# VectorE's exponentials taken from the score tile's third bank, in five passes instead of six

## The chip, the core and the metric

The kernel runs on one core of a Trainium2 chip. The profile names the core's engines PE (TensorE, matrix products; its weight loads are listed apart as PEld), DVE (VectorE), ACT (ScalarE), POOL (GpSimd) and SP (SyncE, which issues the DMAs here). Each engine works through its own list of instructions in order, and the lists are tied together by semaphores: an instruction can carry a wait for another engine's count.

The metric is the device time of one execution in microseconds (us), as the median of three runs. One further execution was recorded by the profiler. Its span is the time from its first to its last instruction, and all durations below come from it.

## The reference

One layer of a transformer over 2,048 tokens of width 640: attention with 32 heads of 20 columns, then a gated product of two linear maps, each behind a layer norm and added to its input. All tensors are bfloat16.

```python
def _A_ref(x, wqkv, wo):
    B, S, D = x.shape            # 1, 2048, 640
    H = 32
    Dh = D // H                  # 20
    q, k, v = ...                # from x @ wqkv, each (B, H, S, Dh)
    scores = jnp.einsum("bhqd,bhkd->bhqk", q, k) * (Dh ** -0.5)
    p = _softmax(scores, axis=-1)
    o = jnp.einsum("bhqk,bhkd->bhqd", p, v)
    return o.transpose(0, 2, 1, 3).reshape(B, S, D) @ wo

def _B_ref(x, w_gate, w_up, w_down):
    return ((x @ w_gate) * (x @ w_up)) @ w_down

h = x + _A_ref(_layernorm(x), A_wqkv, A_wo)
h2 = h + _B_ref(_layernorm(h), B_w_gate, B_w_up, B_w_down)
```

For each head there are 2,048 x 2,048 scores, and each needs an exponential. That is the bulk of the elementwise work.

## The kernel before

**Tiling of the attention.** Scores are computed transposed: 128 keys on the partitions, queries along the columns. Heads go in groups of four (`HPG`), eight groups (`NG`). The four heads of a group lie on four bands of 32 partitions (`SLOT`), so a score product uses 32 rows of the array, and a product with the values writes 32 columns of it. A *segment* (`segs`, L294 to L303) is one group of heads against a block of queries: passes "0", "1", "2" and "3" have 512 queries, passes "A" and "B" 256. For the first four groups of pass "0" the keys come in four chunks (kinds "copy", "add" and "last"); every other segment takes all 16 key blocks in one go (kind "only"). There are 50 segments: 16 chunked ones, 20 unchunked ones of passes "0" to "2", and 14 of passes "3", "A" and "B".

**Score tiles.** The units of work (a key block, a head, 512 or 256 queries) are packed one behind the other into tiles of three banks, 3 x 512 = 1,536 columns (`tiles`, L311 to L324). For tile number i, `emit_S(i)` (L417) writes the scores into a tile `sc` of the pool `scp`, which has two buffers, and then issues one ACTIVATE on ScalarE that turns all 1,536 columns into exponentials in a bfloat16 tile `E` (L433). The finished units join a queue `av_q`, from which `emit_AV` (L568) takes four at a time (eight of 256 columns) and multiplies them with the values into the accumulator `acc` (L597). A column of ones in the values yields the sums of the softmax.

**The main loop** (L1071 to L1100) runs once per tile. It emits, in this order: the scores and exponential of tile i; up to `BUDGET` = 640 ns of the current job's matmuls (`go_on`); the products with the values of a tile some places back; due events and small VectorE work; VectorE's passes for its own exponentials (`step_x`); and, if no job was under way, the start of another job (`begin`). Jobs are the projections to q, k and v, the output projection, the gated product and its down projection. They come from a list in order and write into the one-buffer tile `mi` (`bank()`, L243). The planner keeps an estimate of VectorE's backlog in `now["dve"]`: each instruction adds its supposed cost, and every tile takes `STEP` = 1,331 ns off.

**VectorE's exponentials.** For each of the 20 segments in `X_SEGS` the units of key block 2 are left out of the tile list (L315). Their scores, 80 units of 512 columns, are made apart by `emit_x` (L443) with a matmul into `mi` (L453), in places where a job would otherwise have begun (L1096). VectorE then computes the exponential in six passes: a scaled conversion to an integer that holds exponent and mantissa in its bits (L463), two bit operations that part them (L474, L475), and three multiply-and-add passes (L476, L477, L468). The result `xe` joins `av_q` when all four heads of the segment are done (`put_x`). `need_x` (L496) makes what is missing before a segment closes.

**The constant in the exponent.** A spare row of q and k adds the constant `SHIFT` to all scores. It cancels in the softmax; it places the scores where VectorE's bit arithmetic needs them, and the bias of the ACTIVATE (`EXP_BIAS`) takes it out again. At the end `flag_ok` (L1043) tests the sums' least and greatest value and a saturating conversion, and on a bad outcome the branch `general` computes everything again in a safe way.

Of the kernel before, what the change touches and what calls it, by code (L numbers as in the profile page):

```python
# [3 lines left out]

# [6 lines left out]
BF16 = mybir.dt.bfloat16  # L11
F32 = mybir.dt.float32
I32 = mybir.dt.int32
ACT = mybir.ActivationFunctionType
ALU = mybir.AluOpType
AX = mybir.AxisListType

P = 128
# [26 lines left out]
EPS_B = 1.0013580322265625e-05  # L45
SUM_LO = 1e-15
SUM_HI = 1e15
NEXT = "next slot"
END = "end"
BUDGET = 640  # L50
# [2 lines left out]
LAG = 10  # L53
STEP = 1331
AUX_LOAD, X_LOAD = 1200, 900
SHIFT = 394.0
X_AHEAD, X_STEP, X_OUT = 8, 5, 6
LOG2E = 1.4426950408889634
X_SCALE = SM_SCALE * LOG2E * 2.0 ** 23
C3 = 0.07802454279127117  # L60
X_P, X_Q, X_R = -0.10261439735317812, 6.123365857342997, 5.794771205884579
EXP_BIAS = (SHIFT * SM_SCALE * LOG2E - 127.0) / LOG2E - math.log(C3) - SHIFT * SM_SCALE


@with_exitstack
def kernel(
# [197 lines left out]
    def q_of(g, b, c0, w):  # L264
        return qb[g][:, c0:c0 + w] if b == NB - 1 else qa[g][:, b * QB + c0:b * QB + c0 + w]
# [30 lines left out]
    for ch in range(NB):  # L296
        for g in range(G1):
# [28 lines left out]
    first_tile = {}  # L326
    for i, (us, _) in enumerate(tiles):
        for s, *_ in us:
            first_tile.setdefault(s, i)
    x_todo = deque((first_tile[s] - X_AHEAD + X_STEP * j, s, j) for s in X_SEGS for j in range(HPG))  # L330
    x_pieces = deque()
    x_made = {}
    x_put = []
    x_live = {"units": 0, "passes": 0}

    av_q = deque()
    acc = {"seg": None, "t": None, "from": 0, "left": 0}
# [79 lines left out]
    def emit_S(i):  # L417
        sc = scp.tile([P, EW], F32, name="sc")
        us, n = tiles[i]
        for s, kt, j, _ in us:  # L420
            p, g = segs[s][0:2]
            ensure(("k", g, kt // TPB))
            ensure(("q", PASS[p][0], g))
        for s, kt, j, o in us:
            p, g = segs[s][0:2]
            b, c0, w = PASS[p]
            nc.tensor.matmul(  # L427
                sc[:, o:o + w],
                lhsT=kT[g][SLOT * j:SLOT * (j + 1), kt * P:(kt + 1) * P],
                rhs=q_of(g, b, c0, w)[SLOT * j:SLOT * (j + 1), :],  # L430
                start=True, stop=True)
        e = ep.tile([P, EW], BF16, name="E")
        nc.scalar.activation(e[:, 0:n], sc[:, 0:n], ACT.Exp, bias=EXP_BIAS, scale=SM_SCALE)  # L433
        for s, kt, j, o in us:
            av_q.append((i, s, kt, j, e[:, o:o + PASS[segs[s][0]][2]]))

    def x_ready():
        due, s, _ = x_todo[0]
        p, g = segs[s][0:2]
        return (due <= now["i"] and x_live["units"] < X_OUT and x_live["passes"] < 2  # L440
                and ("q", PASS[p][0], g) in done and ("k", g, 0) in done)

    def emit_x():  # L443

        _, s, j = x_todo.popleft()
        p, g = segs[s][0:2]
        b, c0, w = PASS[p]
        n = BANK // w
        ensure(("k", g, X_KT // TPB))
        ensure(("q", b, g))  # L450
        ps = bank()
        for k in range(n):
            nc.tensor.matmul(  # L453
                ps[:, k * w:(k + 1) * w],
                lhsT=kT[g][SLOT * j:SLOT * (j + 1), (X_KT + k) * P:(X_KT + k + 1) * P],
                rhs=q_of(g, b, c0, w)[SLOT * j:SLOT * (j + 1), :],
                start=True, stop=True)
        v = xp.tile([P, BANK], I32, name="xv", bufs=2)
        m = xp.tile([P, BANK], F32, name="xm")
# [3 lines left out]
        nc.vector.tensor_scalar(v[:], ps[:], X_SCALE, 0.0, ALU.mult, ALU.max)  # L463
        x_live["units"] += 1
        x_live["passes"] += 1

        def last():
            nc.vector.scalar_tensor_tensor(e[:], t[:], X_R, v[:].bitcast(F32), ALU.add, ALU.mult)  # L468
            x_live["passes"] -= 1
            x_made.setdefault(s, []).append((j, e))  # L470
            if len(x_made[s]) == HPG:
                x_put.append([(now["i"], s, X_KT + k, j, e[:, k * w:(k + 1) * w]) for k in range(n) for j, e in x_made[s]])
        x_pieces.extend([
            (430, lambda: nc.vector.tensor_scalar(m[:].bitcast(I32), v[:], 0x007FFFFF, 0x3F800000, ALU.bitwise_and, ALU.bitwise_or)),  # L474
            (430, lambda: nc.vector.tensor_scalar(v[:], v[:], 0x7F800000, None, ALU.bitwise_and)),  # L475
            (690, lambda: nc.vector.scalar_tensor_tensor(t[:], m[:], X_P, m[:], ALU.add, ALU.mult)),  # L476
            (690, lambda: nc.vector.scalar_tensor_tensor(t[:], t[:], X_Q, m[:], ALU.add, ALU.mult)),  # L477
            (690, last)])

    def put_x():  # L480

# [7 lines left out]
    def step_x(n):  # L489
        while n > 0 and x_pieces:  # L490
            ns, fn = x_pieces.popleft()
            dve(ns)
            fn()
            n -= 1

    def need_x(s):  # L496
        while len(x_made.get(s, ())) < HPG:
            if x_pieces:
                step_x(1)
                continue  # L500
            while not cur["fresh"]:
                step()
            emit_x()

    def norm(s, asb):
        p, g = segs[s][0:2]
# [61 lines left out]
    def emit_AV(upto):  # L568
# [21 lines left out]
            return  # L590
        for _ in range(ready):
            _, _, kt, j, e = av_q.popleft()
            if s in X_SEGS and kt == X_KT:
# [448 lines left out]

    def flag_ok():  # L1043
        n = col["n"]
        nc.vector.tensor_reduce(ext[:, 0:1], sums_all[:, 0:n], axis=AX.X, op=ALU.min)
        nc.vector.tensor_reduce(ext[:, 1:2], sums_all[:, 0:n], axis=AX.X, op=ALU.max)
        lo = small.tile([P, 1], F32, name="lo", tag="m32")
        hi = small.tile([P, 1], F32, name="hi", tag="rstd")
        nc.vector.tensor_scalar(lo[:], ext[:, 0:1], SUM_LO, None, ALU.is_ge)
        nc.vector.tensor_scalar(hi[:], ext[:, 1:2], SUM_HI, None, ALU.is_le)  # L1050
        ok = small.tile([P, 1], BF16, name="ok", tag="den")
        nc.vector.tensor_tensor(ok[:], lo[:], hi[:], ALU.mult)
        top = small.tile([P, 1], I32, name="top", tag="nt")
        nc.vector.tensor_scalar(top[:], huge[:], 1.0, 0.0, ALU.mult, ALU.max)
        nc.vector.tensor_scalar(lo[:], top[:], 2.0e9, None, ALU.is_ge)
        nc.vector.tensor_tensor(ok[:], ok[:], lo[:], ALU.mult)
        return ok

# [10 lines left out]
    b_seen, a_seen = 0, False  # L1069
    i = 0  # L1070
    while i < n_tiles or av_q:  # L1071
        now["i"], now["dve"] = i, max(0, now["dve"] - STEP)
        if i < n_tiles:
            emit_S(i)
        if i == first_last:
            for g in range(NG):
                ensure(("spill", g))
# [15 lines left out]
        while x_pieces and now["dve"] < X_LOAD:  # L1093
            step_x(1)
        if not used:
            if x_todo and cur["fresh"] and now["dve"] < X_LOAD and x_ready():  # L1096
                emit_x()
# [106 lines left out]
```

## Time and profile before

| | us |
|---|---|
| median of three runs | 981.02 (979.47 to 981.46) |
| span of the profiled execution | 977.6 |
| TensorE matmuls busy | 865.3 |
| VectorE busy | 576.8 |
| ScalarE busy | 905.2 |
| first exponential starts / last one ends, from the span's start | 16.1 / 933.6 |
| VectorE, six passes of 80 units: L463, L474, L475, L476, L477, L468 | 55.0, 37.4, 35.1, 55.7, 56.3, 56.6 |

A row of the profile's list of groups reads: line, engine, operation, tile written <- tiles read, partitions x elements and type of both, count | total busy us, mean ns of one | idle time of the engine just before them, and whose work ended it. Busy time counts overlapping instructions once, so with the exponentials, which overlap, total busy time is less than count times mean. In the views in order of time a row starts with its start and its length in us, and equal instructions that follow each other are merged into one row with a count.

### The profile page before, as it was taken

The page shows a single profiled execution, that of the slowest core. Times are in us where ns is not written, and L with a number is a line of the kernel's source. Part 1 is how long each engine was busy: PE and PEld are TensorE (multiplying, and loading weights), DVE is VectorE, ACT ScalarE, POOL GpSimd, SP SyncE. Part 2 cuts the span into 40 slices and gives each one's busy share as a digit, 9 for nine tenths or more (in the row PEclk, how much of TensorE's full clock was granted, in tenths as well). Part 3 has the DMA queues.
Part 4 walks back from the last instruction along what each step waited for, and adds up shares of the span by engine and source line. Part 5 has one row for each costly group of instructions (what it writes and reads, how often), then busy time and mean ns, then how long its engine had stood idle before and what let it go on. Part 6 is the DMA issues. An engine that isn't in the chain of part 4 may idle for free.

```text
span 977.6 us, 17623 instructions
## 1 busy us (share of the span) xinstructions
PE 865.3 (89%) x6981; PEld 325.1 (33%) x7041; DVE 576.8 (59%) x1186; ACT 905.2 (93%) x692; POOL 64.6 (7%) x163
## 2 busy tenths in 40 slices
PE   6779998889989899999898988898889999989987
PEld 4223332222223222233232222233332333435455
DVE  7564367877777777777677677777143331143232
ACT  6689999999999899999999999999899999999941
POOL 4110001200000000000000000000000000000000
PEclk9999999999999599999778899999597999989989
DMA  6000000010014022101420222000602000211210
GB/s 182 4 24 1 1 25 24 13 32 27 5 47 146 12 66 59 40 13 33 180 67 12 66 67 60 12 22 23 163 1 66 14 13 20 67 36 40 81 35 17
DMA packets 67816, 44.42 MB, mean 45 GB/s; under 512 B 18504, under 2 KB 63404, under 8 KB 67728
## 3 DMA queue, kind: packets, MB, share of 16 engines
q1 hardware_dynamic: 67728, 43.23, 15.5%
q8 instruction: 57, 0.93, 0.4%
q14 instruction: 31, 0.25, 0.1%
HBM read 35.91 MB, written 7.30 MB: 44 GB/s over the span
## 4 chain that ended last, share of the span: by engine, by line
ACT 44%; PE 32%; issue 13%; DVE 9%; POOL 1%; ACTq 0%; DVEq 0%; POOLq 0%
ACT E L433 44%; PE sc L427 8%; PE acc L597 6%; PE mi L878 3%; PE mi L270 3%; PE mi L812 2%; PE mi L284 2%; PE mi L911 2%; PE f L878 2%; DVE xv L463 1%; PE mi L453 1%; DVE st L176 1%; PE f L911 1%; PE mi L252 1%; DVE vx L239 1%
## 5 line engine op out<-in xcount | busy, mean ns | idle before, releaser
L433 ACT ACTIVATE E<-sc 128x1536 bf16<-128x1536 f32 x656 | 887.8, 1662 | 30.4 <-PE sc L427 29.7
L427 PE MATMUL sc<-qa,kT 32*128 32x512 bf16 x1456 | 205.9, 406 | 41.3 <-ACT E L433 35.0
L597 PE MATMUL acc<-E,vx 128*32 128x512 bf16 (+1 forms) x2352 | 215.6, 374 | 5.3 <-DVE vx L239 4.1
L427 PEld LDWEIGHTS <-kT 32*128 32x128 bf16 x2352 | 89.8, 92 | 260.8 <-issue 251.0
L597 PEld LDWEIGHTS <-vx 128*32 128x32 bf16 x2432 | 56.6, 94 | 159.7 <-issue 151.9
L270 PE MATMUL mi<-lnT,wp 128*128 128x512 bf16 x282 | 84.7, 382 | 9.7 <-DVE kT L277 2.3
L427 PE MATMUL sc<-qb,kT 32*128 32x256 bf16 (+1 forms) x896 | 72.0, 301 | 13.8 <-ACT E L433 13.0
L529 POOL TENSOR_TENSOR on<-asb,bc 128x512 bf16<-128x512 f32 (+1 forms) x30 | 34.5, 1150 | 714.7 <-DMA bc<-scr 507.1
L463 DVE TENSOR_SCALAR xv<-mi 128x512 int32<-128x512 f32 x80 | 55.0, 688 | 29.9 <-PE mi L453 26.3
L911 PE MATMUL mi<-wd,hh 128*128 128x320 bf16 x378 | 68.4, 303 | 3.6 <-DVE xv L463 3.5
L239 DVE CAST u<-mi 128x512 bf16<-128x512 f32 (+3 forms) x56 | 34.9, 624 | 56.2 <-PE mi L878 56.0
L886 DVE TENSOR_TENSOR hh<-mi,u 128x512 bf16<-128x512 f32 (+3 forms) x56 | 34.9, 624 | 55.0 <-PE mi L878 54.9
L878 PE MATMUL mi<-ln2T,wu 128*128 128x512 bf16 (+2 forms) x188 | 55.2, 385 | 4.6 <-DVE xv L463 3.0
L468 DVE SCALAR_TENSOR_TENSOR xe<-xt,xv 128x512 bf16<-128x512 f32 x80 | 56.6, 707 | 2.0
L477 DVE SCALAR_TENSOR_TENSOR xt<-xt,xm 128x512 f32<-128x512 f32 x80 | 56.3, 704 | 0.9
L476 DVE SCALAR_TENSOR_TENSOR xt<-xm 128x512 f32<-128x512 f32 x80 | 55.7, 697 | 0.0
L878 PE MATMUL mi<-ln2T,wg 128*128 128x512 bf16 (+2 forms) x187 | 52.3, 372 | 2.2 <-issue 0.8
L911 PEld LDWEIGHTS <-hh 128*128 128x128 bf16 x448 | 37.5, 97 | 40.1 <-issue 29.8
L915 DVE TENSOR_TENSOR xr<-mi,xr 128x320 bf16<-128x320 f32 x27 | 13.3, 492 | 51.3 <-PE mi L911 51.3
L812 PE MATMUL mi<-wo,on 128*128 128x320 bf16 x224 | 41.8, 311 | 0.7 <-DVE xv L463 0.4
L607 DVE COPY asb<-acc 128x512 f32<-128x512 f32 (+1 forms) x34 | 20.2, 594 | 34.5 <-PE acc L597 32.3
L277 DVE TENSOR_SCALAR kT<-mi,one_row 128x512 bf16<-128x512 f32 x31 | 23.2, 749 | 29.0 <-PE mi L270 29.0
(143 smaller groups left out, 637.0 us busy)
## 6 DMA issues: line engine op xcount, KB each, us to landing
bc<-scr SPq DMA_DIRECT2D x100, 64.0 KB
wu<-in_B_w_up_dram SPq DMA_DIRECT2D x20, 320.0 KB
wg<-in_B_w_gate_dram SPq DMA_DIRECT2D x20, 320.0 KB
qsp<-qa SPq DMA_DIRECT2D x8, 384.0 KB
xr<-in_A_x_dram SPq DMA_DIRECT2D x16, 160.0 KB
out_dram<-xr SPq DMA_DIRECT2D x14, 160.0 KB
wd<-in_B_w_down_dram SPq DMA_DIRECT2D x13, 160.0 KB
xs<-in_A_x_dram SPq DMA_DIRECT2D x3, 640.0 KB
```

The lines of the kernel that those rows point to most:

```text
L239: nc.vector.tensor_copy(dst, src)
L270: nc.tensor.matmul(ps[:], lhsT=wslice(m, g, c), rhs=lnT[:, c, ch * QB:(ch + 1) * QB], start=(c == 0), stop=(c == KT - 1))
L427: nc.tensor.matmul(sc[:, o:o + w], lhsT=kT[g][SLOT * j:SLOT * (j + 1), kt * P:(kt + 1) * P], rhs=q_of(g, b, c0, w)[SLOT * j:SLOT * (j + 1) ...
L433: nc.scalar.activation(e[:, 0:n], sc[:, 0:n], ACT.Exp, bias=EXP_BIAS, scale=SM_SCALE)
L463: nc.vector.tensor_scalar(v[:], ps[:], X_SCALE, 0.0, ALU.mult, ALU.max)
L468: nc.vector.scalar_tensor_tensor(e[:], t[:], X_R, v[:].bitcast(F32), ALU.add, ALU.mult)
L476: (690, lambda: nc.vector.scalar_tensor_tensor(t[:], m[:], X_P, m[:], ALU.add, ALU.mult)),
L477: (690, lambda: nc.vector.scalar_tensor_tensor(t[:], t[:], X_Q, m[:], ALU.add, ALU.mult)),
L597: nc.tensor.matmul(acc["t"][SLOT * j:SLOT * (j + 1), 0:w], lhsT=vx[kt][:, VS * h:VS * h + SLOT], rhs=e, start=(acc["n"][j] == 0), stop=(ac ...
L812: nc.tensor.matmul(ps[:, 0:HALF], lhsT=on[g][:, t * P:(t + 1) * P], rhs=wo[g][:, cs], start=(g == 0), stop=(g == NG - 1))
L878: nc.tensor.matmul(ps[0:M, 0:n], lhsT=st["w", fp][k][:, c, f2 * P:f2 * P + M], rhs=st["ln2T"][:, c, c0:c0 + n], start=(c == 0), stop=(c == ...
L911: nc.tensor.matmul(ps[:, 0:HALF], lhsT=st["hh"][f][0:K, t * P:(t + 1) * P], rhs=late["Wd"][f][0:K, cs], start=(f == 0), stop=(f == 2 * FP ...
```

## The change

Key block 2 is no longer left out: all units are packed into the tiles again. Instead, `emit_S` decides for each tile, by a new function `x_takes`, whether VectorE takes the tile's third bank. It does if the tile is full, lies in one unchunked segment, is at least `X_LEAST` = 4 tiles before that segment's last one, no passes of an earlier unit are still to be issued, VectorE's estimated backlog is under 900 ns, and fewer than six results are outstanding. Then the first pass reads `sc` directly, the ACTIVATE covers the first two banks, 1,024 columns, and the planner books 904 ns for the tile instead of 1,331. Segments of passes "3", "A" and "B" can be chosen too. No unit's scores go through `mi` any more, and job starts are not displaced.

The arithmetic is new as well. `SHIFT` grows from 394 to 1,184 and the first pass leaves a float between 2^15 and 2^16, whose low 15 mantissa bits are the fraction; one bit operation extracts them, and three passes of a cubic add the correction and write the bits of a bfloat16 as a 16-bit integer. So five passes replace six. A result joins `av_q` by itself when it is done. The end flag compares the sums by their bits and saturates to 16 instead of 32 bits.

```diff
-    X_KT = 2
-    X_SEGS = [s for s, (p, g, _, _, kind) in enumerate(segs)
-              if kind == "only" and p in "012"]
...
-            if s in X_SEGS and X_KT <= kt < X_KT + n:
-                continue
...
+        n_act = n
+        if x_takes(i):
+            n_act = n - BANK
+            emit_x(sc[:, n_act:n], [(s, kt, j, o - n_act) for s, kt, j, o in us if o >= n_act])
         e = ep.tile([P, EW], BF16, name="E")
-        nc.scalar.activation(e[:, 0:n], sc[:, 0:n], ACT.Exp, bias=EXP_BIAS, scale=SM_SCALE)
+        nc.scalar.activation(e[:, 0:n_act], sc[:, 0:n_act], ACT.Exp, bias=EXP_BIAS, scale=SM_SCALE)
...
+        return STEP - (n - n_act) * 427 // BANK
+
+    def x_takes(i):
+        us, n = tiles[i]
+        s = us[-1][0]
+        return (n == EW and segs[s][4] == "only" and last_tile[s] - i >= X_LEAST and len({u[0] for u in us}) == 1
+                and not x_pieces and now["dve"] < X_LOAD and x_live["units"] < X_OUT)
...
+    def emit_x(ps, us):
...
+        v = xp.tile([P, BANK], F32, name="xv", bufs=2)
+        m = xp.tile([P, BANK], I32, name="xm")
         t = xp.tile([P, BANK], F32, name="xt")
-        e = xp.tile([P, BANK], BF16, name="xe", bufs=X_OUT)
+        e = xp.tile([P, BANK], I16, name="xe", bufs=X_OUT)
         dve(690)
-        nc.vector.tensor_scalar(v[:], ps[:], X_SCALE, 0.0, ALU.mult, ALU.max)
+        nc.vector.tensor_scalar(v[:], ps, X_SCALE, X_BASE, ALU.mult, ALU.max)
...
+            nc.vector.scalar_tensor_tensor(e[:], t[:], X_C, v[:], ALU.add, ALU.add)
...
+            x_put.append([(now["i"], s, kt, j, e[:, o:o + w].bitcast(BF16)) for s, kt, j, o in us])
...
+            (430, lambda: nc.vector.tensor_scalar(m[:], v[:].bitcast(I32), 0x7FFF, 0x8000, ALU.bitwise_and, ALU.bitwise_or)),
+            (700, lambda: nc.vector.scalar_tensor_tensor(t[:], m[:], X_A, m[:], ALU.mult, ALU.mult)),
+            (700, lambda: nc.vector.scalar_tensor_tensor(t[:], t[:], X_B, m[:], ALU.add, ALU.mult)),
+            (700, last)])
...
-            if x_todo and cur["fresh"] and now["dve"] < X_LOAD and x_ready():
-                emit_x()
-            else:
-                begin(START)
+            begin(START)
```

More of the change, by code (lines that the diff above doesn't have):

```diff
@@ L55 @@
 AUX_LOAD, X_LOAD = 1200, 900
-SHIFT = 394.0
-X_AHEAD, X_STEP, X_OUT = 8, 5, 6
+X_LEAST, X_OUT = 4, 6
+SHIFT = 1184.0
 LOG2E = 1.4426950408889634
[L59 to L62, printed above, removed]
+X_UNIT = 128.0
+X_BASE = 32768.0
+X_SCALE = SM_SCALE * LOG2E * X_UNIT
+C0, C1, C3 = 0.45805436, 0.46569895, 0.07629467
+X_A = X_UNIT * C3 / X_BASE ** 3
+X_B = X_UNIT * (C1 - 1.0) / X_BASE
+X_C = X_UNIT * C0 - X_BASE
+EXP_BIAS = -(X_BASE / X_UNIT + 127.0) / LOG2E
 @with_exitstack
@@ L324 @@
         tiles.append((cur_t, pos))
[L326 to L330, printed above, removed]
+    last_tile = {s: i for i, (us, _) in enumerate(tiles) for s, *_ in us}
     x_pieces = deque()
-    x_made = {}
+    x_left = {}
     x_put = []
-    x_live = {"units": 0, "passes": 0}
+    x_live = {"units": 0}
+    x_last = set()
     av_q = deque()
@@ L437, in x_ready @@
[L437 to L459, printed above, removed]
+            if o < n_act:
+                av_q.append((i, s, kt, j, e[:, o:o + PASS[segs[s][0]][2]]))
@@ L460, in emit_x @@
         t = xp.tile([P, BANK], F32, name="xt")
-        e = xp.tile([P, BANK], BF16, name="xe", bufs=X_OUT)
+        e = xp.tile([P, BANK], I16, name="xe", bufs=X_OUT)
         dve(690)
-        nc.vector.tensor_scalar(v[:], ps[:], X_SCALE, 0.0, ALU.mult, ALU.max)
+        nc.vector.tensor_scalar(v[:], ps, X_SCALE, X_BASE, ALU.mult, ALU.max)
         x_live["units"] += 1
-        x_live["passes"] += 1
+        x_left[s] = x_left.get(s, 0) + 1
         def last():
[L468 to L472, printed above, removed]
@@ L496, in need_x @@
     def need_x(s):
[L497 to L502, printed above, removed]
-            emit_x()
+        while x_left.get(s):
+            step_x(1)
     def norm(s, asb):
@@ L592, in emit_AV @@
             _, _, kt, j, e = av_q.popleft()
-            if s in X_SEGS and kt == X_KT:
+            if (s, kt, j) in x_last:
                 x_live["units"] -= 1
@@ L1068 @@
     first_last = next(k for k, (us, _) in enumerate(tiles) if PASS[segs[us[0][0]][0]][0] == LAST_B)
-    b_seen, a_seen = 0, False
+    b_seen, a_seen, took = 0, False, 0
     i = 0
     while i < n_tiles or av_q:
-        now["i"], now["dve"] = i, max(0, now["dve"] - STEP)
+        now["i"], now["dve"] = i, max(0, now["dve"] - took)
         if i < n_tiles:
-            emit_S(i)
+            took = emit_S(i)
+        elif x_pieces:
+            step_x(len(x_pieces))
         if i == first_last:
```

28 lines of the change are left out of this document (14 added, 14 removed).

## The prediction

> **What bounds the kernel now.** First the page's busy shares, then the groups by form, then who waits for whom, then one stretch in order of time.
>
> ```profile
> PE 865.3 (89%) x6981; PEld 325.1 (33%) x7041; DVE 576.8 (59%) x1186; ACT 905.2 (93%) x692; POOL 64.6 (7%) x163
> ...
> L433 ACT ACTIVATE E<-sc 128x1536 bf16<-128x1536 f32 x656 | 887.8, 1662 | 30.4 <-PE sc L427 29.7
> ```
>
> ScalarE (ACT) is busy 93% of the span, nearly all of it with 656 exponentials of 1,536 columns. They overlap: the mean of one is 1.662 us, but 887.8/656 = 1.353 us each, and in undisturbed stretches their ends stand 1.343 us apart (588 of 655 distances in the trace). ACT sits idle before them for only 30.4 us.
>
> ```profile
> PE sc L427 <- ACT E L433: 48.0, 123, 1.0
> ...
> ACT E L433 <- PE sc L427: 29.7, 38, 4.7
> ```
>
> The waits (us, times, longest) show a loop of two score tiles. TensorE (PE) waits 123 times for ACT to release one, and ACT waits 38 times for PE, with 36 us lost between first and last exponential beyond 1.343 us a tile. So ACT sets the pace and PE is close behind. The stretch that decides my price:
>
> ```profile
> 211.25 8.28 ACT L433 ACTIVATE E<-sc 128x1536 bf16<-128x1536 f32 x6
> ...
> 212.60 0.69 DVE L463 TENSOR_SCALAR xv<-mi 128x512 int32<-128x512 f32 x1 [0.40 <-PE mi L453]
> ...
> 214.21 0.39 PE L427 MATMUL sc<-qa,kT 32*128 32x512 bf16 x3
> ...
> 215.55 0.39 PE L427 MATMUL sc<-qa,kT 32*128 32x512 bf16 x3
> ...
> 216.96 0.39 PE L427 MATMUL sc<-qa,kT 32*128 32x512 bf16 x3
> ```
>
> The six exponentials end at 219.53; stepping back by 1.343, earlier ones end at 215.50, 216.84 and 218.19. The scores of the following tiles were complete at 214.60, 215.94 and 217.35. So a tile lies ready 0.90, 0.90 and 0.84 us before ACT's preceding exponential ends. I call this the lead. Over tiles 87 to 655 of the trace it has median 0.83 and mean 0.70 us; without the 5% under 0.1 us, where ACT waited for PE, the mean is 0.76; 46% are over 0.85. It cannot grow much past 0.90, because the scores start when the exponential two tiles back ends (215.55 follows 215.50).
>
> **Fewer and more on ACT.** The 80 units of before were left out of the tile list, 80 x 512/1536 = 26.7 tiles. They return: 683 tiles instead of 656. In the program as built, 117 tiles are cut to 1,024 columns, and the last tile has 1,024 as well; 565 stay full. What 512 columns are worth comes from the line's own view and two groups by form:
>
> ```profile
> L433 ACT ACTIVATE E<-sc x656: 1445/1624/2108, 16.1 to 932.1; 128x1536 bf16<-128x1536 f32 x164
> ```
>
> ```profile
> L236 ACT CAST u<-f 128x256 bf16<-128x256 f32 x13 | 4.9, 377 | 8.7 <-PE f L878 7.8 <-DVE hh L886 0.9
> ...
> L691 ACT ACTIVATE kT<-sc,one_row 128x512 bf16<-128x512 f32 x1 | 0.7, 687 | 0.3 <-PE sc L657 0.3
> ```
>
> From 256 to 1,536 columns: (1445 - 377)/1280 = 0.834 ns a column, 0.427 us for 512. Bounds: 0.379 from the 687 ns row, 0.448 as a third of 1.343. I take 0.427, since its rows lie furthest apart. ACT's work is 683 x 1.343 - 118 x 0.427 = 866.9 us against 656 x 1.343 = 881.0: **-14.1 us** (-8.6 to -16.7). Of the 117 units, 89 lie in the 20 groups that had 80, and 28 in the last 14 groups, which had none. In the first part ACT has 27 more tiles for 9 more units; the gain sits in the second part.
>
> **The new wait.** In the program as built each of the 117 short ACTIVATEs waits for VectorE (DVE), for pass xv of its own tile; full ones wait for TensorE. So ACT cannot read the first two banks until DVE has read the third. Behind the waiting ACTIVATE stand only further exponentials; its E tile feeds acc, and its sc tile the scores two tiles on, so PE waits next. The path: scores complete; xv starts 0.037 us later if DVE is free (0.036 to 0.038 where the old one found it idle); xv takes 0.688 (L463); DVE to ACT takes 0.085 (of the five such hand-overs in the trace three take 0.084 to 0.094, two 0.033); the short exponential alone takes 1.445 - 0.427 = 1.018. That ends 1.828 us after the scores. Unhindered it would end 1.343 - 0.427 = 0.916 after its predecessor. So a stall is 1.828 - 0.916 = 0.912 us, less the lead, plus what xv waits in DVE's queue.
>
> ```profile
> L463 DVE TENSOR_SCALAR xv<-mi 128x512 int32<-128x512 f32 x80 | 55.0, 688 | 29.9 <-PE mi L453 26.3 <-PE sc L427 3.2
> L474 DVE TENSOR_SCALAR xm<-xv 128x512 int32<-128x512 int32 x80 | 37.4, 468 | 2.7
> L475 DVE TENSOR_SCALAR xv<-xv 128x512 int32<-128x512 int32 x80 | 35.1, 439 | 2.8
> ```
>
> Queue: the old xv found DVE idle for 54 of its 80 (49 and 5 waits); from its own matmul's end to its start it took 0.128 us on average, 0.397 at the 90th percentile, so 0.09 extra. After: the order on DVE puts an evacuation and then xe (0.707) ahead of xv for 19 of 117, and an evacuation with three passes behind it over two tiles for 13; these some 32 wait about 0.6 us, 0.17 on average. I take 0.13, between the two. With lead 0.76 the stall is 0.28, with 0.70 it is 0.34; I take 0.29, nearer the first because where ACT waited for PE anyway the stall is partly absorbed. 117 x 0.29 = **+33.9 us**. Bounds of a stall: 0.01 (lead 0.90, empty queue) and 0.61 (lead 0.70, queue 0.40), so +1 to +71 us.
>
> The Trainium skill, "PSUM — Partial Sum Buffer", section "PSUM bank collisions raise a hardware error", wants order between two engines only on the same bank and quadrant; reads of different banks run side by side. By that rule no such wait is needed, and without it the sum would stop at -14.1 us. The trace of before has no case of two engines reading one sc tile.
>
> **The rest.** DVE's own work: before 80 x (688 + 468 + 439 + 697 + 704 + 707) = 296 us, after 117 x (688 + 468 + 697 + 704 + 707) = 382 us (the new passes by the old ones of their kind). DVE rises to some 662 us of 997, 66%; covered, except through the queue above. PE: the same number of score and acc matmuls; 80 scores move from lone ones into threes (about 11 us less, 53 fewer turns of 0.21), while acc calls that meet one head twice rise from 20 to 65 of full width (45 x 0.21 = 9 us more, half the 0.42 between 0.61 and 1.03 us that one such call shows at half clock). I cost both at nothing; PE's 112 us of idle time cover them; without cover, 9 us. The mi bank is free of units: PE lost 9.5 us to xv there; I take 0 because ACT, not mi, sets the pace (0 to -9.5). Job slots rise, 27 tiles and 80 slots, so the work queue is dry in 160 iterations instead of 64. Where it was dry TensorE's clock was 0.50 (480 to 498 us), scores took 0.61 instead of 0.39 and the lead was 0.68: a stall of 0.23 and queue, no dearer than my mean. The end flag swaps types only. DMA issues keep their number (302 rows on SP), shifted with their groups; on POOL one multiply moves. The 44.0 us after the last exponential stay.
>
> **Sum.** 977.6 - 14.1 + 33.9 = 997.4 us of span. The median of the runs, 981.0, is 3.4 above the profiled span: **1001 us**, 2% slower.
>
> **Rivals.** *The wait is covered* (faster): ACT waits, but scores are early and DVE free. The point that decides is a stall of 14.1/117 = 0.12 us. For it: 46% of leads are over 0.85, and 54 of 80 old passes found DVE idle. Against: the mean lead alone leaves 0.15 before any queue. At 0.05 us: 977.6 - 14.1 + 5.9 + 3.4 = 973. If ACT did not have to wait at all, 977.6 - 14.1 + 3.4 = 967; that gets 0.02 of this case's chance, since the built program has the wait. It is what the Trainium skill's page on PSUM, named above, would allow.
> *DVE's queue decides*: evacuations that wait for PE jobs stand ahead of xv more often than I count; at 0.61 us, 977.6 - 14.1 + 71.4 + 3.4 = 1038. For it: 32 such places; against: a new unit starts only when the previous one's passes are all issued.
> *PE becomes the bound* (busy 818.7 of the 917.5 us from 16.1 to 933.6): a cut brings nothing and every tile costs the present 1.353: 27 x 1.353 = 36.5 more, 1017.5. Against: PE waits 48 us for ACT now.
> *It does not do what it says*: the new type of the flag sends the run into the general branch, 16 x 8 x 4 pairs of exponentials of 1.445 and 0.687, over 1,090 us more.
>
> **How the numbers follow.** Forecast (stall 0.20 to 0.45, 990 to 1020 us) 0.50; covered 0.20; DVE's queue 0.17; PE 0.07; general branch 0.01; a stall near 0.12, no change, 0.05. No change means within 0.2%, about what a measurement of this kernel can tell. So faster 0.20, same 0.05, slower 0.75. The range is 969 to 1040: it takes in half or more of the covered case and of the queue's.
>
> **What would show it.** Right: 117 short exponentials released by DVE xv, idle time before them near 30 us; full ones still 1.34 apart; DVE near 660 us. Wrong: short ones that start with no gap (then 0.916 after their predecessor and a span near 965 to 970), or gaps over 0.5 us with xe or an evacuation running, or gaps released by PE. The price fails if leads after differ much from 0.76.

## The result and the profile after

The changed kernel takes **1,022.83 us** (median of four runs, 1,020.82 to 1,024.4) against 980.25 (977.18 to 981.46) for the kernel before in the same session: ratio **1.0443**, 95% interval 1.0416 to 1.047. The forecast was 1,001. Direction and mechanism came out as forecast; the loss of 42.6 us is a little over twice the forecast 20.

The page of the changed kernel: busy time by engine, the granted TensorE clock in 40 slices of 25.5 us (tenths of full speed), and the chain of waits by engine.

```profile
PE 899.9 (88%) x6985; PEld 328.5 (32%) x7041; DVE 659.8 (65%) x1291; ACT 901.6 (88%) x719; POOL 65.6 (6%) x163
...
PEclk9989998999767999965568999965587999989989
...
PE 47%; DVE 24%; ACT 17%; issue 10%; POOL 1%; ACTq 0%; DVEq 0%; POOLq 0%
```

The last two rows of the kernel before, for comparison:

```profile
PEclk9999999999999599999778899999597999989989
...
ACT 44%; PE 32%; issue 13%; DVE 9%; POOL 1%; ACTq 0%; DVEq 0%; POOLq 0%
```

ScalarE's share of the span falls from 93% to 88%: it is no longer nearly full. The chain that ended last, of which ScalarE held 44% before, now runs through TensorE and VectorE. There are more slices with 5 and 6 in the clock's row than before; they come back below. Below, *half-clock time* is the part of the span in which TensorE's granted clock was 0.50.

The groups by form (count | busy us, mean ns | idle before, and who ended it):

```profile
L434 ACT ACTIVATE E<-sc 128x1536 bf16<-128x1536 f32 x565 | 775.7, 1481 | 24.9 <-PE sc L424 24.2 <-PE acc L582 0.2
...
L434 ACT ACTIVATE E<-sc 128x1024 bf16<-128x1024 f32 x118 | 120.8, 1023 | 54.6 <-DVE xv L455 51.2
...
L455 DVE TENSOR_SCALAR xv<-sc 128x512 f32<-128x512 f32 x117 | 80.4, 687 | 82.1 <-PE sc L424 81.3
```

ScalarE is idle 54.6 us before the 118 short exponentials, and VectorE's pass xv ended nearly all of it. Idle time before full ones fell from 30.4 to 24.9 us. The list of waits (us, times, longest) has the same story with its count:

```profile
PE sc L424 <- ACT E L434: 58.6, 150, 1.1
...
ACT E L434 <- DVE xv L455: 51.2, 83, 4.6
...
ACT E L434 <- PE sc L424: 24.2, 28, 2.8
```

From the records of the single instructions I made a ledger: the time from the first exponential's start to the last one's end is a floor (1.343 us for each full tile, 0.916 for each short one, and the first) plus stalls, the excess of each distance between two ends over that.

| us | before | after | difference |
|---|---|---|---|
| floor | 881.1 | 867.0 | -14.1 |
| stalls before short tiles | - | 66.8 (117 x 0.571) | +66.8 |
| stalls before full tiles, first 86 tiles / the rest | 15.0 / 21.4 | 15.6 / 13.7 | -7.1 |
| ahead of the first and behind the last exponential | 60.1 | 58.5 | -1.6 |
| span | 977.6 | 1021.6 | +44.0 |

The 66.8 and the 54.6 of the groups agree: a short exponential that had to wait takes 1.023 us alone, where one that follows its predecessor closely adds 0.916, so 54.6 + 117 x 0.107 = 67.1.

One stretch in order of time shows a stall (start, length, then the row as before):

```profile
373.97 4.13 ACT L434 ACTIVATE E<-sc 128x1536 bf16<-128x1536 f32 x3
...
375.31 0.69 DVE L245 CAST u<-mi 128x512 bf16<-128x512 f32 x1 [1.43 <-PE mi L863]
...
375.92 0.68 DVE L466 SCALAR_TENSOR_TENSOR xt<-xm 128x512 f32<-128x512 int32 x1
...
376.64 0.69 DVE L467 SCALAR_TENSOR_TENSOR xt<-xt,xm 128x512 f32<-128x512 f32 x1
...
376.95 0.39 PE L424 MATMUL sc<-qa,kT 32*128 32x512 bf16 x3
...
377.36 0.69 DVE L460 SCALAR_TENSOR_TENSOR xe<-xt,xv 128x512 int16<-128x512 f32 x1
...
377.97 0.68 DVE L455 TENSOR_SCALAR xv<-sc 128x512 f32<-128x512 f32 x1
...
378.57 0.68 DVE L871 TENSOR_TENSOR hh<-mi,u 128x512 bf16<-128x512 f32 x1
378.75 7.74 ACT L434 ACTIVATE E<-sc 128x1024 bf16<-128x1024 f32 x6 [0.64 <-DVE xv L455]
...
379.30 0.59 PE L863 MATMUL mi<-ln2T,wu 128*128 128x512 bf16 x2 [0.75 <-DVE hh L871]
```

ScalarE's last row merges the short exponential with five full ones behind it. The scores of the short tile are ready at 377.34, and the preceding exponential ends at 378.10: a lead of 0.76, as forecast. But VectorE, held up by a job's u that waited 1.43 us for TensorE, still has the old unit's xt, xt and xe to do, so xv starts 0.63 us after the scores, and ScalarE idles for 0.64. Behind xv stands the job's hh, and TensorE's next job matmul waits 0.75 us for it: the delay goes on.

### The profile page after: what moved, and what is told of

Its sections match the earlier page's. It is cut to its first block, busy times and chain, and to the rows that moved or that the text cites. A ratio compares the mean times of both kernels' runs of the same rounds, so it can differ in the third digit from the quotient of the medians.

```text
span 1021.6 us, 17772 instructions
## 1 busy us (share of the span) xinstructions
PE 899.9 (88%) x6985; PEld 328.5 (32%) x7041; DVE 659.8 (65%) x1291; ACT 901.6 (88%) x719; POOL 65.6 (6%) x163
## 4 chain that ended last, share of the span: by engine, by line
PE 47%; DVE 24%; ACT 17%; issue 10%; POOL 1%; ACTq 0%; DVEq 0%; POOLq 0%
ACT E L434 17%; PE sc L424 12%; PE acc L582 9%; PE mi L863 7%; PE mi L896 5%; DVE xv L455 4%; PE mi L276 4%; DVE xe L460 3%; DVE xt L467 3%; PE mi L797 2%; DVE xt L466 2%; PE mi L290 2%; DVE hh L871 2%; PE f L863 2%; DVE st L182 1%
## 5 line engine op out<-in xcount | busy, mean ns | idle before, releaser
L434 ACT ACTIVATE E<-sc 128x1536 bf16<-128x1536 f32 (+1 forms) x683 | 884.2, 1402 | 79.6 <-DVE xv L455 51.2
L424 PE MATMUL sc<-qa,kT 32*128 32x512 bf16 x1536 | 233.5, 444 | 57.1 <-ACT E L434 50.2
L582 PE MATMUL acc<-E,vx 128*32 128x512 bf16 (+1 forms) x2294 | 244.3, 397 | 4.0 <-DVE vx L245 3.3
L455 DVE TENSOR_SCALAR xv<-sc 128x512 f32<-128x512 f32 x117 | 80.4, 687 | 82.1 <-PE sc L424 81.3
L582 PEld LDWEIGHTS <-vx 128*32 128x32 bf16 x2432 | 61.7, 96 | 168.7 <-issue 161.4
L467 DVE SCALAR_TENSOR_TENSOR xt<-xt,xm 128x512 f32<-128x512 f32 x117 | 85.8, 733 | 3.0
L514 POOL TENSOR_TENSOR on<-asb,bc 128x512 bf16<-128x512 f32 (+1 forms) x30 | 35.8, 1195 | 764.7 <-DMA bc<-scr 569.9
L460 DVE SCALAR_TENSOR_TENSOR xe<-xt,xv 128x512 int16<-128x512 f32 x117 | 82.4, 704 | 2.8
L466 DVE SCALAR_TENSOR_TENSOR xt<-xm 128x512 f32<-128x512 int32 x117 | 82.8, 708 | 1.7
L465 DVE TENSOR_SCALAR xm<-xv 128x512 int32<-128x512 int32 x117 | 56.8, 485 | 2.4
L582 PE MATMUL acc<-xe,vx 128*32 128x512 bf16 (+1 forms) x138 | 53.4, 412 | 0.0
```

Of the source, the lines that this page charges most:

```text
L424: nc.tensor.matmul(sc[:, o:o + w], lhsT=kT[g][SLOT * j:SLOT * (j + 1), kt * P:(kt + 1) * P], rhs=q_of(g, b, c0, w)[SLOT * j:SLOT * (j + 1) ...
L434: nc.scalar.activation(e[:, 0:n_act], sc[:, 0:n_act], ACT.Exp, bias=EXP_BIAS, scale=SM_SCALE)
L455: nc.vector.tensor_scalar(v[:], ps, X_SCALE, X_BASE, ALU.mult, ALU.max)
L460: nc.vector.scalar_tensor_tensor(e[:], t[:], X_C, v[:], ALU.add, ALU.add)
L465: (430, lambda: nc.vector.tensor_scalar(m[:], v[:].bitcast(I32), 0x7FFF, 0x8000, ALU.bitwise_and, ALU.bitwise_or)),
L466: (700, lambda: nc.vector.scalar_tensor_tensor(t[:], m[:], X_A, m[:], ALU.mult, ALU.mult)),
```

## The experiments

Ratios are to the kernel before, run beside each kernel on the same chip. All diffs are against the changed kernel unless another is named.

**No units at all.** VectorE computes no exponentials; ScalarE does all 683 tiles.

```diff
     def x_takes(i):
+        return False
```

> The changed kernel, but no tile is cut: ScalarE does all 683 tiles (the last one with 1,024 columns) and VectorE computes no exponentials. Theory A (the short ACTIVATE waits for pass xv of its own tile, and that stall eats the cut): ScalarE's floor rises to 682 x 1.343 + 0.916 = 916.8 us from the 866.9 of the changed kernel, but its 66.8 us of stalls at short tiles vanish; with some 25 to 36 us of other stalls the time is 1004 to 1015, so 8 to 19 us FASTER than the changed kernel although VectorE's 117 units are gone. Rival B (TensorE is the bound, because 27 tiles come back and job starts are no longer displaced): the pace is TensorE's, which has the same products to do, so the time stays at 1020 to 1030. Rival C (the units do pay, only less than hoped): slower than the changed kernel, 1030 to 1070.

Measured: 1,011.16 us, ratio 1.0339 (1.029 to 1.0389). The group of all but the last exponential:

```profile
L434 ACT ACTIVATE E<-sc 128x1536 bf16<-128x1536 f32 x682 | 921.3, 1731 | 28.5 <-PE sc L424 26.6 <-PE acc L582 1.4
```

No wait on VectorE is left, and the time falls by 12 us although ScalarE gets 117 x 512 columns more. The floor rises to 916.9 and the stalls fall to 33.0 in all. So the 117 units, worth 50 us of ScalarE's time, cost more than they save.

**The same wait the other way round.** The ACTIVATE is issued ahead of xv, so that ScalarE reads first and VectorE waits.

```diff
-        n_act = n
-        if x_takes(i):
-            n_act = n - BANK
-            emit_x(...)
+        n_act = n - BANK if x_takes(i) else n
         e = ep.tile([P, EW], BF16, name="E")
         nc.scalar.activation(e[:, 0:n_act], sc[:, 0:n_act], ...)
+        if n_act < n and tiles[i][1] == EW:
+            emit_x(...)
```

> The changed kernel with the ACTIVATE issued ahead of xv: the order between the two readers of a cut tile turns round, xv waits for the short exponential, and ScalarE waits only for TensorE. Theory A: idle time of ScalarE before short tiles released by VectorE goes from 51 us to nothing; but xv now starts about 1.6 us after the scores, holds VectorE's queue that long, and gives the tile back some 0.8 us late to the scores two tiles on, whose lead falls from 0.9 to about 0.1; a full tile stalls by 0.21 less its lead, plus what evacuations lose. The time is between 995 and 1020. Rival B (TensorE's pace): no change, 1020 to 1026.

Measured: 1,064.98 us, ratio 1.089 (1.0811 to 1.0968), a miss. Its waits:

```profile
DVE xv L454 <- ACT E L431: 164.3, 111, 6.0
...
ACT E L431 <- PE sc L424: 101.5, 143, 4.1
...
PE mi L862 <- DVE hh L870: 27.3, 33, 1.4
...
PE sc L424 <- DVE xv L454: 23.0, 37, 1.3
```

The stalls before short tiles are nearly gone (10.0 us in the ledger), but those before full tiles rise to 128.5. xv now starts 1.40 us after the scores; jobs wait behind it on VectorE (27.3), the next scores wait for the tile that it holds (23.0), and ScalarE waits for scores 143 times. The shared tile orders the two readers either way, and what waits second is worse off with VectorE, which has jobs behind it.

**The unit's scores in a bank of their own.** They go to `mi` again, in the same turn as the tile, only where no job is under way: 91 short tiles.

```diff
+        n_act = n - BANK if cur["fresh"] and x_takes(i) else n
+        ps = bank() if n_act < n else None
...
-                sc[:, o:o + w],
+                sc[:, o:o + w] if o < n_act else ps[:, o - n_act:o - n_act + w],
...
+            emit_x(ps[:], ...)
```

> The changed kernel, but the scores of a cut tile's third bank go into the one-buffer tile mi instead of sc, so that the two readers share no tile; a tile is cut only when no job holds mi, which leaves 91 cut tiles instead of 117. Theory A: no short ACTIVATE waits for VectorE any more; ScalarE's floor is 682 x 1.343 + 0.916 - 91 x 0.427 = 878 us, with 30 to 40 us of stalls as before the change, so 970 to 982 us, near the kernel before. Rival B (TensorE's pace, 27 more tiles, denser jobs): at least 1005.

Measured: 1,048.1 us, ratio 1.0717 (1.064 to 1.0795), a miss again. Its waits:

```profile
ACT E L434 <- PE sc L426: 90.3, 90, 3.9
...
PE mi L863 <- DVE xv L455: 16.9, 28, 0.8
```

ScalarE's wait on VectorE is gone (3.1 us of stalls before short tiles), but a job that starts in the same turn needs `mi`, so TensorE stands behind xv and the next scores are late. It was repaired by starting no job in such a turn, with units in passes "0" to "2" alone. That leaves 72 units; the 73 in the expectation, and in the second group below, counts the last tile, which has 1,024 columns anyway:

```diff
-        if not used:
+        if not used and (i >= n_tiles or took == STEP):
             begin(START)
```

> As e3_own_bank (the unit's scores in mi, so no tile with two readers), but in an iteration with a cut tile no new job is started, as the kernel before did it, and only in passes 0 to 2: 73 cut tiles. In e3_own_bank the next job's matmul stood in TensorE's queue behind the unit's xv, ahead of the next scores (PE mi <- DVE xv 28 us), and ScalarE waited 90 us for scores. Theory A (with the shared tile gone and mi not fought over, the cuts are worth their 0.427 us): ScalarE's floor is 916.9 - 73 x 0.427 = 885.8, with some 33 to 40 us of stalls, 977 to 992. Rival B (TensorE's pace forbids it: 27 more tiles): no better than the kernel without units, 1005 to 1020.

Measured: 992.16 us, ratio 1.0131 (1.0103 to 1.0158), 0.2 us above the expected range.

```profile
L434 ACT ACTIVATE E<-sc 128x1536 bf16<-128x1536 f32 x610 | 838.4, 1534 | 33.1 <-PE sc L426 31.5 <-PE acc L582 0.2
L434 ACT ACTIVATE E<-sc 128x1024 bf16<-128x1024 f32 x73 | 77.3, 1059 | 0.3 <-PE sc L426 0.3
```

Short tiles now start without a gap: 0.3 us of idle time in all. TensorE no longer waits for xv ahead of a job (28.5 us in all in the kernel of 91, nothing here); two things were changed at once, so which of them did it is not separated. Against the kernel without units the floor falls by 30.7 us and the time by 19.0. So units do pay where nobody waits for them. But 72 units with 683 tiles save ScalarE less than the 80 before that took 26.7 tiles out of the list: the floor is 5.1 us above that of the kernel before, the stalls are 43.7 us against 36.4, and the kernel before stays ahead.

**Two tiles in place of one.** The score tile is split into two banks (`sa`) and one (`sb`), each from its own pool, with two ACTIVATEs for a full tile. VectorE reads `sb`, ScalarE `sa`; the units are the same 117. A twin has no units.

```diff
-        sc = scp.tile([P, EW], F32, name="sc")
+        sa = scp.tile([P, 2 * BANK], F32, name="sa")
+        sb = sc3.tile([P, BANK], F32, name="sb")
...
+        nc.scalar.activation(e[:, 0:n2], sa[:], ACT.Exp, bias=EXP_BIAS, scale=SM_SCALE)
+        if n_act > n2:
+            nc.scalar.activation(e[:, n2:n_act], sb[:, 0:n_act - n2], ACT.Exp, bias=EXP_BIAS, scale=SM_SCALE)
```

> The changed kernel with the score tile split: banks one and two in a tile sa, bank three in a tile sb (two buffers each, the same six banks), so a cut tile's readers share nothing. Full tiles then need two ACTIVATEs, 1,024 and 512 columns. By the 1.343 us between ends, 1,536 columns at 0.834 are 1.281 and 0.062 goes with each instruction, so the floor is 866.9 + 565 x 0.062 = 902 us. Theory A: no stall before the 117 cut tiles, so 902 plus 30 to 45 us elsewhere and 61 us at the ends: 993 to 1010, and about 117 x (0.427 + 0.062) = 57 us, at least 35, less than its twin without units. Rival B (TensorE's pace): less than 15 us between the twins.

> The twin of e8_two_tiles: score tile split in two, but no tile is cut, ScalarE does everything in two ACTIVATEs per tile; VectorE computes no exponentials. Floor 916.9 + 682 x 0.062 = 959 us, with 20 to 33 us of stalls and 61 us at the ends: 1040 to 1055. With the shared tile, leaving out all units made the kernel 12 us faster (1011 against 1023); with the split tile theory A expects it to make it at least 35 us slower. Rival B: within 15 us of e8_two_tiles.

Measured: 1,014.88 us with units (ratio 1.0363, 1.0338 to 1.0387), above the expected range, and 1,046.92 without (1.069, 1.0661 to 1.0719). With a tile of its own for VectorE the same units bring 32.0 us; with the shared tile they cost 11.7 (1,022.83 against 1,011.16). 32 falls just short of the 35 that the first theory asked for. Part of it belongs to the split: a cut tile here also saves its second ACTIVATE. The ends of full tiles stand 1.407 us apart and a cut one adds 0.917 (medians), so a cut saves 0.490 us instead of 0.427, 57 us for 117, of which about 7 are the second ACTIVATE. Of the 25 us between 57 and 32, ScalarE's longer wait for scores is 19.5. First the kernel with units, then its twin:

```profile
ACT E L437 <- PE sb L427: 38.7, 58, 4.3
```

```profile
ACT E L437 <- PE sb L427: 19.2, 25, 3.5
```

**A later start of the next unit.** A new unit starts only two tiles after the last pass of the one before was issued: 102 short tiles.

```diff
-                and not x_pieces and now["dve"] < X_LOAD ...)
+                and not x_pieces and i - x_live.get("last", -9) >= 2 and now["dve"] < X_LOAD ...)
...
             x_left[s] -= 1
+            x_live["last"] = now["i"]
```

> The changed kernel, but a tile is cut only two or more tiles after the last pass of the unit before was issued, so that xv rarely stands right behind xe in VectorE's queue; 102 cut tiles instead of 117. Theory A, with the two terms as the trace of the changed kernel has them (stall 0.912 less a lead of 0.56 plus 0.21 of queue): the queue term falls to 0.05 or less, the stall to about 0.38, and ScalarE's time is 916.8 - 102 x 0.427 + 102 x 0.38 and 29 us elsewhere, some 22 us less than in the changed kernel: 996 to 1006. If the queue is not what makes the stall (only the late scores are): 15 short tiles fewer at a stall of 0.57, about 1020.

Measured: 1,008.63 us, ratio 1.0314 (1.0261 to 1.0366), a little above the expected range. In its waits:

```profile
ACT E L434 <- DVE xv L455: 28.4, 66, 1.6
```

xv waits 0.093 us in VectorE's queue on average instead of 0.209, the stall falls from 0.571 to 0.424 us a short tile, 43.2 us in all. The lead hardly moves (0.563 to 0.595).

**TensorE kept busy.** In turns without a job two spare matmuls, whose result nobody uses, go to `mi`.

```diff
+            dry = not jobs and not urgent and cur["gen"] is None
             begin(START)
+            if dry and 40 <= i < n_tiles:
+                ps = bank()
+                for _ in range(2):
+                    nc.tensor.matmul(ps[:], lhsT=ident[:], rhs=kT[0][:, 0:BANK], start=True, stop=True)
```

> The changed kernel with two spare matmuls of 512 columns on TensorE in each turn after tile 40 in which no job is left (about 160 turns, 0.43 us each at full clock, result unused), so that TensorE is not idle there. In the changed kernel TensorE had half its clock for 250 us, in stretches with no job left; 34 of the 117 short tiles lay there, with a mean lead of 0.445 us instead of 0.611. Theory A (the stall before short tiles comes from the shared tile's wait whatever the clock): half-clock time falls below 150 us, the 34 tiles gain at most 0.17 us each, 6 us, and the full ones some of their 14 us of stalls; 1008 to 1022 us. Rival B (the slow clock is what made the stalls twice as large as forecast): stalls fall from 67 to near 40 us in all and the time to 985 to 1005. Rival C (spare work takes TensorE's time from the scores): slower than 1023.

Measured: 1,011.06 us, ratio 1.0341 (1.0324 to 1.0359), 11.8 us below the changed kernel. Its page and its waits:

```profile
PEclk9988999999997999999997999999997999989999
```

```profile
ACT E L434 <- DVE xv L455: 45.4, 72, 1.8
```

The low slices are gone: half-clock time falls from 247 to 66 us (the 250 of the expectation, like the 130 further down, counts some 3 us behind the span's end). The spare products ran in 124 turns, not in the 160 expected. The lead of short tiles rises from 0.563 to 0.668 us, their stall falls to 0.490 (57.3 us in all), and the later full tiles' stalls from 13.7 to 7.1. All of the short tiles' gain lies where the clock was slow. The 34 tiles that had half clock gain 0.28 us each (lead 0.445 to 0.803, stall 0.536 to 0.256), while the other 83 stay as they were (lead 0.611 and 0.612, stall 0.585 and 0.586). So the slow clock was a part of the loss, more than the 6 us that the first theory gave it on short tiles (9.4), but not most of it.

**Both mended.** The later start and the spare matmuls together.

> The kernel of 102 short tiles in which a new unit starts only two tiles after the last pass of the one before (queue 0.09 us, lead 0.60 us, stall 0.42 us a short tile, 1008.6 us), with the two spare matmuls in turns without a job (they brought the changed kernel a lead of 0.67 us). Theory (a stall is 0.912 us less the lead plus the queue, and the two inputs can be mended one by one): lead 0.65 to 0.70, stall 0.30 to 0.36, near the 0.29 that was forecast; the short tiles' stalls fall from 43 to 31 to 37 us, those of full tiles by 3 to 7: 990 to 1000 us. Rival (the sum hides another cost of the shared tile): the stall stays at 0.40 or more, 1001 to 1009 us.

Measured: 997.56 us, ratio 1.0197 (1.017 to 1.0225).

```profile
ACT E L434 <- DVE xv L455: 25.4, 55, 1.6
```

Lead 0.661, queue 0.096: the prediction's sum gives 0.912 - 0.661 + 0.096 = 0.347 us a short tile, and 0.361 was measured (36.8 us for 102). The same sum gives 0.558 for the changed kernel (0.571 measured), 0.410 with the later start (0.424), 0.476 with the spare matmuls (0.490). It holds within 0.014 us four times, so the stall stays below the rival's 0.40, and the queue and the lead could be mended one by one. This is no independent proof of the sum, since its terms add up to the measured distance: what it shows is that its constant part, xv with its hand-over and the short exponential, is the same in all four. A cost of the units that works through the lead is not ruled out by it.

**The old place.** Four kernels without the shared tile. First the kernel before with only the new arithmetic (five passes, new constants, new end flag):

> The kernel before with the new arithmetic alone: the 80 units in the old place (own scores in mi, key block 2), five passes instead of six, the new constant and flag. VectorE's work falls by 80 x 0.439 = 35 us, but it is not the bound (577 of 978 us busy). Theory A: within 0.5% of the kernel before, 974 to 982, so none of the 42 us comes from the arithmetic. A rival (the new passes, with integer operands or an integer result, cost more or come out late): over 985.

Measured: 982.41 us, ratio 1.0032 (1.0016 to 1.0049). One pass less of VectorE's time is worth nothing there; it is 0.3% slower, so in that place the arithmetic costs at most some 5 of the 42 us (the upper end of the interval). Then the same with 88 units instead of 80 (against the kernel before):

```diff
-              if kind == "only" and p in "012"]
+              if kind == "only" and p in "0123"]
```

> Not the shared tile at all: the kernel before with the five new passes, units made through the one-bank tile mi in the old place, and two more segments, those of the pass with key 3, added, 88 units instead of 80. Eight units are worth 2.67 tiles of 1.343 us, 3.6 us. Theory A: 974 to 981 us, that is 0 to 6 below the kernel before. Rival (units in the later part displace jobs that the end waits for): 984 to 995.

Measured: 977.21 us, ratio 0.9991 (0.9971 to 1.0011): no difference from the kernel before. Then the spare matmuls alone, in the kernel before:

> The kernel before with the two spare matmuls alone, in its some 60 turns without a job. It had half clock for 130 us and 21 us of stalls after tile 86. Theory A: half-clock time falls below 80 us, but ScalarE set the pace there too, so the time falls by 0 to 8 us, 973 to 981. Rival B (the slow clock costs most of the 21 us): below 970. Rival C (the spare work delays scores): above 982.

Measured: **974.31 us**, ratio **0.9965** (0.9948 to 0.9982), the one version clearly faster than both kernels, by 0.35%. The spare products ran in 25 turns, not in the 60 expected. Half-clock time falls from 127 to 93 us, less than expected, and the stalls after tile 86 from 21.4 to 15.9. The 88 units together with the spare matmuls:

> The kernel of 88 units in the old place (977.2 us beside 977.9 for the kernel before) with the two spare matmuls in turns without a job, which alone brought the kernel before to 974.3. If both add: 970 to 975 us, faster than the kernel before by 0.3 to 0.8%. Rival (the eight units fill the same turns that the spare work would): 975 to 979.

Measured: 977.26 us, ratio 0.9997 (0.9981 to 1.0013), a miss: no gain is left. Its half-clock time fell from 127 to 93 us as well, and the spare products ran in 22 turns, so the eight units did not fill those turns, as the rival has it; but its stalls did not fall (19.0 to 19.8 after tile 86). Why is open. The spare matmuls in the kernel of 72 units with their own bank:

> The kernel of 73 short tiles whose units' scores lie in a bank of their own and which starts no job in the same turn (992 us), with the two spare matmuls in turns without a job. It has no wait before short tiles left; its waits are ScalarE's for scores, 32 us. Theory A (part of these lies where TensorE has half its clock): 976 to 988 us. Rival (they come from units and jobs that meet in mi): 989 to 1000.

Measured: 986.98 us, ratio 1.0107 (1.0051 to 1.0163). That is inside the expected range, but a gain is not shown: the interval takes in that of the kernel without them (1.0103 to 1.0158). Half-clock time fell from 186 to 80 us, yet the stalls after tile 86 did not (24.3 to 25.1), so there the slow clock was not what ScalarE waited for.

## Why the prediction was right and wrong

**What bounds the kernel** was read rightly: the floor by ScalarE's work fell by the forecast 14.1 us (881.1 to 867.0), and full exponentials still end 1.343 us apart (median; 510 of 564 within 0.006).

**The new wait** was right in place and form. Each short ACTIVATE waits for xv of its own tile; xv took 0.687 us (forecast 0.688), the hand-over to ScalarE 0.093 (0.085), the short exponential 1.023 (1.018). With these values the constant of the sum is 0.924, where the forecast had 0.912. The Trainium skill, "PSUM — Partial Sum Buffer", section "PSUM bank collisions raise a hardware error", asks for order only on the same bank and quadrant; the wait row of 51.2 us shows that this program is ordered by the tile. A build without that order was not tried; separate tiles were, and there no ScalarE wait on xv is left.

**The step that failed is the size: "I take 0.29".** The stall was 0.571 us, 117 x 0.281 = 32.9 us more than the 33.9 forecast. Two inputs were off.

*The lead was 0.563 us, not 0.76.* I took the mean of the leads before without the 5% under 0.1 us, though with them it was 0.70, as if those would be absorbed. The full tiles of the kernel without units have 0.719, so 0.70 was the number to take. And I took the stretches without jobs as "no dearer than my mean", from one place with a lead of 0.68. That was the usual value there, not the mean: in the trace of before, over the 67 tiles from number 87 on whose scores were made at half clock, the mean lead was 0.27 us, against 0.75 at full clock.

After the change 34 of the 117 short tiles lay where TensorE had half its clock, with a lead of 0.445; the other 83 had 0.611. Half-clock time grew from 127 to 247 us: I had counted the dry turns (64 to 160) and not followed what they do to the clock. VectorE's units are not what makes it longer, since the kernel without units has 267 us of it. The spare matmuls show the part of the clock: 9.4 us of stalls before short tiles, all on those 34, and 6.6 us before full ones after tile 86 (2.6 were lost before it), with the whole time 11.8 lower.

The rest of the 32.9, some 23 us, lies on the 83 tiles at full clock, where the lead is 0.611 with spare matmuls or without, and the queue is longer (next paragraph). In the kernel without units the same 83 tiles have 0.751. There TensorE's products into `mi` wait 15.6 us in all for VectorE, in the changed kernel 36.3. So VectorE's passes may hold up the jobs, and the jobs the scores behind them; no run tested this alone, and it stays open.

*The queue was 0.209 us, not 0.13.* 69 of 117 xv started at once; the other 48 started 0.53 us after their scores on average, and 40 of these stood behind xe of the unit before. I had counted 32 places from the order. The queue lay where jobs ran: 0.272 us on the 83 tiles at full clock, 0.054 on the 34 at half clock, so a short tile at half clock stalled no longer than another (0.536 against 0.585). The planner starts a unit when the passes of the last one are issued, not when they are done. The later start brought the queue to 0.093.

**What made up for part of it.** Stalls before full tiles fell by 7.1 us, which I had at nothing; the part after tile 86 fell from 21.4 to 13.7. The stretch around the exponentials fell by 1.6, and the median lies 1.2 above the profiled span instead of 3.4. Together 997.4 + 32.9 - 7.1 - 1.6 = 1021.6.

**The rest.** VectorE was forecast at some 662 us and was busy for 659.8. The bounds of ScalarE's term come to -8.5 and -16.6, not -8.6 and -16.7, which changes nothing. **The rivals:** *the wait is covered* fell, with 7 of 117 stalls under 0.12 us. *VectorE's queue decides* had nearly the right stall (0.61), but its reason gave the smaller part: 0.08 us of the 0.28 missing, against 0.20 from the lead. *TensorE becomes the bound* fell as worded, since cuts do bring ScalarE their 0.427 us and full tiles wait less. In the two kernels that took ScalarE's wait for VectorE away by other means ScalarE waited for scores instead (101.5 and 90.3 us), but there TensorE itself stood behind VectorE, so they do not show TensorE as a bound of its own. The run stayed far from *the general branch*.

**The sign** followed from a narrow account: 14.1 us of gain over 117 tiles bears a stall of 0.12. With both inputs mended the stall is 0.36 and the ratio still 1.0197.

## What to carry to other kernels

Before an engine takes over part of a tile that the bounding engine also reads, price the wait as hand-over plus its pass less the lead, once for each tile, and set that against what one such tile saves; with a separate buffer for the second reader the same units brought 32 us instead of costing 12, each against its own twin, though splitting the tile cost 36 us here. Take the lead as the mean over all tiles of a stretch, apart for full and half clock and for stretches with and without jobs, and follow a change that empties a job queue to TensorE's clock. Look at what stands behind an instruction before letting it wait: moving this wait to VectorE cost another 42 us.

## What the runs showed that was not expected

TensorE's clock falls to 0.50 without long pauses. In the changed kernel it stood at half from 672 to 747 us, where the records of its matmuls leave 16% of the time idle and no gap is longer than 0.87 us. That 16% is counted at half clock, at which three score products take 0.61 us instead of 0.39. In the last 3.4 us at full clock, before 672, TensorE was idle 50% of the time, in gaps of up to 1.15 us; before eight of the nine falls of the clock between 100 and 940 us it was 40 to 51%, before the ninth 87%. These turns hold almost only scores (32 rows of the array) and products with the values (32 columns). Two spare matmuls on 128 rows and 128 columns, at most 0.43 us a turn at full clock, keep the clock up: from 430 to 565 us it was 0.67 and became 0.96, while TensorE's busy time there rose only from 112.4 to 122.9 of 135 us. The Trainium skill, "TensorE: Matmul & The Clock Gate", section "Why this matters for your kernels", advises to avoid idle gaps above about 3 us; here the clock stayed at half with gaps under a third of that, and it fell after gaps of at most 1.2 us at eight of the nine places. In the kernel before, the idle share ahead of the ten falls between 100 and 940 us ran from 23 to 64%, so no threshold can be read from it. Whether the idle share or the used part of the array decides was not tested.

Splitting an exponential in two costs little: 682 tiles in two ACTIVATEs instead of one took 35.8 us more (1,046.92 against 1,011.16 without units), 0.052 us for each split; between the ends of undisturbed tiles it is 0.064 (1.407 against 1.343).
